# A retention block and two MoE layers on one core: the first layer by Strassen's algorithm over blocks of 768 tokens, all attention placed in front of it, and the weights' lowest three bits made by ScalarE from bytes

## The chip, the core and the metric

The kernel runs on 1 core of one Trainium2 chip. The metric is device time of one execution in microseconds (us). The core's engines are PE (TensorE: matmuls, with PEld for its weight loads), DVE (VectorE), ACT (ScalarE), POOL (GpSimd) and SP (SyncE), which issues most of the DMAs here.

## The reference

Three stages follow each other, over 2304 tokens of 512 features (4 sequences of 576 tokens, 8 heads of 64):

```python
def _attn_ref(q, k, v):
    scores = scale * np.matmul(q, k.transpose(0, 1, 3, 2))
    ...
    Dmat = np.where(rel >= 0, gamma[:, None, None] ** rel[None, :, :], 0.0)
    return np.matmul(scores * Dmat, v)

def _moe_ref(x, w_gate, w_val, w_out, rms_g):      # layer A: 512 -> 1536 -> 512
    rms = np.sqrt(np.mean(x * x, axis=-1, keepdims=True) + 1e-06)
    xn = x / rms * rms_g
    g = xn @ w_gate
    silu = g * (1.0 / (1.0 + np.exp(-g)))
    return silu * (xn @ w_val) @ w_out

def _moe2_ref(x, w_in, w_out):                     # layer B: 512 -> 2048 -> 512
    h = x @ w_in
    g = np.where(h >= 1, h, np.where(h <= -1, 0.0, (h + 1) ** 2 / 4))
    return g @ w_out
```

The weights arrive as float64 and are made into float32 on the chip.

## The kernel before

**Matmuls.** A float32 product is made of three matmuls in the type fp32r (`three`): every operand is cut into a rounded part hi and a rest lo, and hi·hi, lo·hi and hi·lo are summed in PSUM. Cutting (`split`) costs one ACT cast and one DVE subtraction. Attention and the norm's sums use plain fp32 matmuls; each shows as two records in the trace.

**Attention** (`scores`, `values`) goes through 20 chunks: per sequence four of 128 tokens and a tail of 64. It keeps a running state for each sequence, which DVE adds to and the next chunk reads. POOL makes the scaled q and k (`qs`, `ks`) and two sums of squares (`sq`, `sum`) for each chunk. The first chunks run in front; the other 13 are put between the matmuls of layer A by `att_step`, one half of a chunk after each front product.

**Layer A** runs in `BLOCKS` of 512, 512, 384, 512 and 384 tokens, with 12 steps (`step_a`) each, one for 128 of the 1536 hidden columns. A step has 24 front matmuls (gate and value: 2 outputs x 4 pieces of 128 features x 3) and, for the step before, 12 back matmuls, all as wide as the block. That makes 60 steps. In block 0 `weights_f32` converts three slots of weights for each step and stores them as float32 in DRAM; later blocks load them back, and every step splits them again.

**Conversion** (`convert`) of a slot of 128x512 weights: an ACT Prelu takes the high words, DVE shifts the result left by 3 (TENSOR_SCALAR), and DVE ors in the top three bits of the low word (SCALAR_TENSOR_TENSOR).

**Layer B** runs in three blocks of 768 tokens with 8 steps (`step_b`) each by Strassen's algorithm in Winograd's form: 2x2 blocks (384 tokens, two 128-column tiles, two halves of 256 features) take 7 products instead of 8, 42 matmuls of 384 columns, and 36 back matmuls of 512. Its weights' seven combinations are prepared during layer A (`prepare_in`, `prepare_out`) and loaded from DRAM.

**Order.** `Plan` records every operation and issues them in an order of its own: it steps through a schedule with costs for each operation, takes on PE the first ready operation in program order, and on the other engines the one due first. What runs on the chip is then that order on each engine, with semaphores for the real dependences. The lines below set what a step of layer A can wait for (two buffers for float32 weights, two for split ones, three staging slots) and when a new chunk of attention is begun.

```python
    w_p = pool("w", 2)
    wt_p = pool("wt", 2)
    stages = [stage_p.tile([P, DM, 2], U32, tag="stage", name="st") for _ in range(STAGE)]
    ...
        elif nscored[0] < min(len(chunks), goal + 1) and nscored[0] == nvalued[0]:
            scores(tags)
```

Of the kernel before, what the change touches and what calls it, by code (L numbers as in the profile page):

```python
# [12 lines left out]
U32 = mybir.dt.uint32  # L13
ACTF = mybir.ActivationFunctionType
# [6 lines left out]
P = 128  # L21
# [8 lines left out]
BLOCKS = [512, 512, 384, 512, 384]  # L30
STARTS = [sum(BLOCKS[:i]) for i in range(len(BLOCKS))]
TB = 384
NSB = NT // (2 * TB)
NPB = NB // 2
MT = 2 * TB // P
EPS = 1e-6
WARM = 16
AHEAD = 3
NORM = NA - 3
ATT = 3  # L40
STAGE = 3
PREPARE = [(), (1, 3, 5, 7), (5, 7), (1, 3, 5, 7), (0, 1, 2, 3, 5, 6)]
# [18 lines left out]
class Plan:  # L61
# [49 lines left out]
    def take(self, engine, real, method, args, kwargs):  # L111
# [10 lines left out]
        for ap, write in [(a, False) for a in ins] + [(out, True)]:  # L122
# [89 lines left out]
def moe_chain_kernel(ctx: ExitStack, tc: tile.TileContext, att, tail, wa, wb, dmat, gq, gk, out):  # L212
    nc = Plan(tc.nc)
    pool = lambda name, bufs, **k: Ring(ctx.enter_context(tc.tile_pool(name=name, bufs=1, **k)), bufs)

    const = pool("const", 1)
    att_p = pool("att", ATT)
    qk_p = pool("qk", 1)
    ret_p = pool("ret", 1)
    stage_p = pool("stage", STAGE)  # L220
    w_p = pool("w", 2)
    wt_p = pool("wt", 2)
    one_p = pool("one", 1)
    h_p = pool("h", 3)
    xraw_p = pool("xraw", 2)
    t_p = pool("t", 2)
    r_p = pool("r", 1)
    sum_p = pool("sum", 2)
    sq_p = pool("sq", 1)
    ps_p = pool("ps", 1, space=PSUM)  # L230
    fr_p = pool("fr", 2, space=PSUM)
    dram_p = pool("dram", 1, space=DRAM)
    d_sb = const.tile([P, H, CH], F32, name="d_sb")
    gq_sb = const.tile([P, NPAIR * (S - CH)], F32, name="gq_sb")
    gk_sb = const.tile([P, NFULL * H + KD], F32, name="gk_sb")
    rg_sb = gk_sb[:, NFULL * H:]
    eps = const.tile([P, 1], F32, name="eps")
    ones = const.tile([P, P], F32, name="ones")
    ones_r = const.tile([P, P], F32R, name="ones_r")
    state = const.tile([P, NPAIR, P], F32, name="state")  # L240
    o_sb = one_p.tile([P, 2 * DM], F32, name="o")
# [12 lines left out]

    def need(t):
        end = STARTS[t] + BLOCKS[t]
        return sum(b * S + c * CH < end for b in range(B) for c in range(NCH))


    slots = [wa[f, :, j * DM:(j + 1) * DM] for f in range(NA) for j in range(3)]  # L260
    slots += [wb[p, k, j] for p in range(NPB) for k in range(2) for j in range(2)]
    stage_t, loaded, taken = {}, [0], [0]
    stages = [stage_p.tile([P, DM, 2], U32, tag="stage", name="st") for _ in range(STAGE)]
    more = [*stages, *(a.rearrange("p (n w) -> p n w", w=2) for a in (wpair_w, wsum_w))]
    stage_of = [more[i % len(more)] if 9 <= i < 3 * NA - 2 else stages[i % STAGE] for i in range(len(slots))]

    def load_slot():
        i = loaded[0]
        if i < len(slots):
            st = stage_of[i]  # L270
            assert all(st is not b for b in stage_t.values())
# [26 lines left out]
    w32_t, wt_t = {}, {}  # L298

    def weights_f32(s):  # L300

        if s >= len(steps):
            return
        f = steps[s][2]
        w = w32_t[s] = w_p.tile([P, 3 * DM], F32, tag="w", name="w")
        if s < NA:
            convert(w, 3)
            nc.sync.dma_start(out=wa32[f], in_=w)
        else:
            nc.sync.dma_start(out=w, in_=wa32[f])  # L310

    def weights_split(s, part):
        if s >= len(steps):
            return
        if part == 0:
            wt_t[s] = wt_p.tile([P, 14 * 2 * P], F32R, tag="wt", name="wt") if s + 1 < len(steps) else wprep
        q = slice(0, 2 * DM) if part == 0 else slice(2 * DM, 3 * DM)
        hi, lo = wt_t[s][:, :3 * DM], wt_t[s][:, 3 * DM:6 * DM]
        split(w32_t[s][:, q], hi[:, q], lo[:, q])

    def a_weights(s, j):
        hi, lo = wt_t[s][:, :3 * DM], wt_t[s][:, 3 * DM:6 * DM]
        return hi[:, j * DM:(j + 1) * DM], lo[:, j * DM:(j + 1) * DM]

    def prepare_in(p):

        convert(wpair, 2)
        n = 2 * P
        a11, a12, a21, a22 = (wpair[:, i * n:(i + 1) * n] for i in range(4))
        s2, s1, s3, s4 = (wsum[:, i * n:(i + 1) * n] for i in range(4))  # L330
# [4 lines left out]
        ready = wprep[:, :14 * n]  # L335
# [4 lines left out]
        nc.sync.dma_start(out=wfd[p], in_=ready.bitcast(F32))  # L340

    def prepare_out(p):
        convert(wpair, 2)
        hl = wprep[:, :4 * DM].rearrange("p (f w n) -> p f w n", f=2, w=2)
        split(wpair.rearrange("p (f n) -> p f n", f=2), hl[:, :, 0], hl[:, :, 1])
        for f in range(2):
            nc.sync.dma_start(out=wod[p, f], in_=wprep[:, f * 2 * DM:(f + 1) * 2 * DM].bitcast(F32))

    prepared = [0]

    def prepare():
        i = prepared[0]
        if i < 2 * NPB:
            (prepare_out if i % 2 else prepare_in)(i // 2)
            prepared[0] += 1

    chunks = [(b, c) for b in range(B) for c in range(NCH)]
    first, ahead = need(0), need(0) + AHEAD  # L360
# [167 lines left out]
    def split_x(t, k0, k1):  # L528
# [9 lines left out]
        if k1 == KD:  # L538
            del xraw[t]
# [351 lines left out]
```

## Time and profile before

| | |
|---|---|
| median of 3 runs | 920.0 us (919.15 to 921.18) |
| the profiled execution | span 920.9 us, granted TensorE clock 0.998 of full speed |
| PE busy | 904.3 us, 98% of the span |
| DVE busy | 576.2 us (63%): between 20 and 340 us 78 to 97% of each 20 us, in layer B 32 to 69% |
| ACT busy | 482.3 us (52%) |
| POOL busy | 70.3 us, all in the first 400 us |
| DMA | 209.9 MB, mean 228 GB/s; 397 GB/s in the busiest stretch |

The span of the profiled execution stands 0.9 us above the median of the runs. PE's busy time counts matmuls that wait in the pipeline as well, so 98% does not mean that no faster order exists; it means that after the opening hardly a gap is left, and that time is decided by what PE is given to do.

### The profile page before, as it was taken

To read this page: it belongs to the slowest core of one execution; us is meant where nothing else is said; L and a number is where in the kernel's file an instruction comes from. 1 tells how busy PE (TensorE), PEld (TensorE's weight loads), DVE (VectorE), ACT (ScalarE), POOL (GpSimd) and SP (SyncE) were. 2 spreads that over 40 slices of the span, in tenths; PEclk is the share of its full clock that TensorE was granted. 3 is DMA by queue.
4 is the path that set the end of the run, shared out by engine and by line. 5 is a ranking of instruction groups with operands and counts; after the bars stand their busy time and mean duration, and the time that the engine had idled before them with its cause. 6 is when DMAs were issued, how large, how long until landed. Compare 5 with 4: busy or idle time off the path is not lost.

```text
span 920.9 us, 13342 instructions
## 1 busy us (share of the span) xinstructions
PE 904.3 (98%) x5098; PEld 797.7 (87%) x5098; DVE 576.2 (63%) x929; ACT 482.3 (52%) x858; POOL 70.3 (8%) x80
## 2 busy tenths in 40 slices
PE   8799999999999999999999999999999999999998
PEld 7578888888889998888899998989888998989896
DVE  3978888888988888855658645434734345434343
ACT  3446665555765576533545454445654455644443
POOL 4620001310014001100000000000000000000000
PEclk9999999999999999999999999999999999999999
DMA  9679976988769984642254386646765454755432
GB/s 364 229 261 314 308 278 235 331 331 325 283 240 378 387 291 150 234 150 94 103 202 153 104 329 243 216 160 216 251 222 194 169 191 170 266 165 213 159 137 69
DMA packets 51647, 209.94 MB, mean 228 GB/s; under 512 B 5632, under 2 KB 11392, under 8 KB 47488
## 3 DMA queue, kind: packets, MB, share of 16 engines
q1 hardware_dynamic: 45392, 199.51, 61.2%
q10 hardware_dynamic: 6192, 9.59, 2.8%
q8 instruction: 40, 0.66, 0.3%
q14 instruction: 23, 0.19, 0.1%
HBM read 167.14 MB, written 41.94 MB: 227 GB/s over the span
## 4 chain that ended last, share of the span: by engine, by line
PE 92%; DVE 4%; DMA 2%; ACT 2%; issue 1%; ACTq 0%
PE fr L135 50%; PE acc L135 31%; PE at L135 11%; DMA out_dram<-o 1%; DMA att<-in_att_dram 1%; DVE xraw L135 1%; DVE xall L135 0%; DVE t L135 0%; DMA gk_sb<-in_gk_dram 0%; DVE w L135 0%; DVE wt L135 0%; ACT att L135 0%; DVE state L135 0%; DVE wsum L135 0%; DVE wpair L135 0%
## 5 line engine op out<-in xcount | busy, mean ns | idle before, releaser
L135 PE MATMUL fr<-xall,wt 128*128 128x384 f32 (+1 forms) x2424 | 512.1, 356 | 3.6 <-DVE xall L135 1.3
L135 PEld LDWEIGHTS fr<-xall,wt 128*128 128x128 f32 x2424 | 436.8, 188 | 53.5 <-DVE xall L135 2.4
L135 PE MATMUL acc<-h,wt 128*128 128x512 f32 (+1 forms) x708 | 158.1, 370 | 0.1
L135 PE MATMUL acc<-wprep,h 128*128 128x512 f32 x576 | 155.7, 394 | 0.5 <-ACT h L135 0.5
L135 PEld LDWEIGHTS acc<-h,wt 128*128 128x128 f32 x708 | 128.4, 188 | 18.2 <-ACT o L135 0.6
L135 DVE TENSOR_TENSOR wt<-w,wt 128x512 fp32r<-128x512 f32 (+1 forms) x118 | 114.4, 985 | 17.7 <-ACT wt L135 17.3
L135 PEld LDWEIGHTS acc<-wprep,h 128*128 128x128 f32 x576 | 106.6, 188 | 15.8 <-ACT h L135 0.9
L135 ACT CAST wt<-w 128x512 fp32r<-128x512 f32 (+1 forms) x118 | 96.7, 835 | 42.1 <-PE acc L135 23.6
L135 DVE TENSOR_TENSOR t<-fr,t 128x512 f32<-128x512 f32 (+1 forms) x120 | 76.3, 636 | 58.0 <-PE fr L135 29.5
L135 ACT ACTIVATE att<-att 128x384 f32<-128x384 f32 x156 | 79.2, 523 | 30.1 <-DVE att L135 18.2
L135 ACT CAST h<-t 128x512 fp32r<-128x512 f32 (+1 forms) x60 | 34.6, 577 | 79.3 <-DVE t L135 79.3
L135 DVE TENSOR_TENSOR att<-fr,att 128x384 f32<-128x384 f32 x48 | 26.6, 555 | 70.6 <-ACT att L135 69.6
L135 PE MATMUL at<-wprep,h 128*128 128x512 f32 x288 | 70.3, 392 | 0.0
L135 DVE TENSOR_TENSOR h<-att,h 128x384 fp32r<-128x384 f32 x96 | 52.8, 554 | 23.7 <-ACT h L135 23.1
L135 ACT ACTIVATE t<-fr 128x512 f32<-128x512 f32 (+1 forms) x60 | 33.3, 554 | 59.0 <-PE fr L135 58.7
L135 PEld LDWEIGHTS at<-wprep,h 128*128 128x128 f32 x288 | 53.7, 188 | 10.4
L135 ACT COPY att<-fr 128x384 f32<-128x384 f32 x48 | 23.0, 479 | 75.7 <-PE fr L135 70.2
L135 ACT CAST h<-att 128x384 fp32r<-128x384 f32 x96 | 48.7, 512 | 21.2 <-DVE att L135 20.0
L135 DVE SCALAR_TENSOR_TENSOR att<-att,att 128x384 f32<-128x384 f32 x48 | 26.8, 558 | 42.3 <-ACT att L135 42.3
L135 DVE TENSOR_TENSOR h<-t,h 128x512 fp32r<-128x512 f32 (+1 forms) x60 | 38.0, 634 | 14.2 <-ACT h L135 13.9
L135 DVE SCALAR_TENSOR_TENSOR att<-att,fr 128x384 f32<-128x384 f32 x24 | 13.3, 553 | 36.8 <-ACT att L135 36.8
L135 DVE TENSOR_TENSOR xall<-xraw,xall 128x512 fp32r<-128x512 f32 (+2 forms) x32 | 25.9, 828 | 2.8 <-ACT xall L135 2.4
(144 smaller groups left out, 672.5 us busy)
## 6 DMA issues: line engine op xcount, KB each, us to landing
w<-wa SPq DMA_DIRECT2D x48, 768.0 KB, 4.5
wprep<-wod SPq DMA_DIRECT2D x48, 512.0 KB, 4.0
wt<-wfd SPq DMA_DIRECT2D x24, 1024.0 KB, 5.2
wt<-wfd SPq DMA_DIRECT2D x24, 768.0 KB, 4.5
stage<-in_wb_dram SPq DMA_DIRECT2D x32, 512.0 KB, 6.4
wfd<-wprep SPq DMA_DIRECT2D x8, 1792.0 KB, 7.0
att<-in_att_dram SPq DMA_DIRECT2D x26, 512.0 KB, 5.8
stage<-in_wa_dram SPq DMA_DIRECT2D x26, 512.0 KB, 5.5
```

Of the source, the lines that this page charges most:

```text
L135: call = lambda: getattr(real, method)(*args, **kwargs)
```

## The change

- **Layer A in 768-token blocks, by the algorithm of layer B.** There are 3 blocks of 12 steps. A step makes gate and value together by 7 products (42 matmuls of 384 columns), and its back part is 12 matmuls of 512 columns and 12 of 256, in accumulators that are 768 tokens wide (`acc0` to `acc3`, and the halves of `at0` and `at1`).
- **Weights of layer A** are prepared like those of layer B: in block 0 each step converts its three slots, makes four sums, splits seven combinations into the buffer `wt` and stores the split ones (1792 KB) and the plain out-weights (256 KB); blocks 1 and 2 load them.
- **Attention in front**, with sequences taken in pairs (0 and 1, then 2 and 3, chunk by chunk in turn). The state of a sequence adds up in a PSUM bank (`fr0`, `fr1`) and ACT copies it out, so DVE adds no more to it. x of the first 768 tokens stays on the chip; x of the others goes to DRAM (`x1d`) and comes back once in each block.
- **Conversion**: ACT makes the low word's top three bits from its top byte (Identity with scale and a bias, written over the staged low words), and one DVE operation shifts and ors. The TENSOR_SCALAR is gone.
- **Silu** replaces Sigmoid and one multiplication. Sums for the norm are made with all three blocks in or just behind the front, so ACT loads its tables 4 times in place of 11.
- **Layer B** keeps its steps. The weights of its steps 3, 5 and 7 (`LATE`) are converted and split within its own first block, the others during blocks 1 and 2 of layer A.

```diff
-BLOCKS = [512, 512, 384, 512, 384]
-PREPARE = [(), (1, 3, 5, 7), (5, 7), (1, 3, 5, 7), (0, 1, 2, 3, 5, 6)]
+ATT = 6
+LATE = (3, 5, 7)
...
-            nc.vector.tensor_scalar(out=q, in0=q, scalar1=3, scalar2=None, op0=ALU.logical_shift_left)
-            nc.vector.scalar_tensor_tensor(
-                out=q, in0=st[:, :, 0], scalar=29, in1=q, op0=ALU.logical_shift_right, op1=ALU.bitwise_or
-            )
+        for q, st in parts:
+            low = st.bitcast(U8).rearrange("p n (w b) -> p n w b", w=2)[:, :, 0, 3]
+            nc.scalar.activation(out=st[:, :, 0], in_=low, func=ACTF.Identity, scale=2.0 ** -5, bias=half)
+            nc.vector.scalar_tensor_tensor(
+                out=q, in0=q, scalar=3, in1=st[:, :, 0], op0=ALU.logical_shift_left, op1=ALU.bitwise_or
+            )
             load_slot()
...
+    def prepare_front(ready, dst):
+        convert(wpair_w)
...
         nc.vector.tensor_add(out=s1, in0=a21, in1=a22)
         nc.vector.tensor_sub(out=s2, in0=s1, in1=a11)
         nc.vector.tensor_sub(out=s3, in0=a11, in1=a21)
         nc.vector.tensor_sub(out=s4, in0=a12, in1=s2)
...
+    def prepare_a(s):
+        prepare_front(wts[s % 2], None)
+        w = w32o[s % 2]
+        convert(w)
+        w = w.bitcast(F32)
+        split(w, wos[s % 4][:, :DM], wos[s % 4][:, DM:])
...
+    def store_a(s):
+        nc.sync.dma_start(out=wfa[s], in_=wts[s % 2].bitcast(F32))
+        nc.sync.dma_start(out=woa[s], in_=w32o[s % 2].bitcast(F32))
...
-    chunks = [(b, c) for b in range(B) for c in range(NCH)]
+    chunks = [(b, c) for pair in ((0, 1), (2, 3)) for c in range(NCH) for b in pair]
...
             for h in range(2):
                 r = slice(h * D, (h + 1) * D)
-                if c:
-                    nc.vector.tensor_add(out=state[r, :, r], in0=state[r, :, r], in1=new[r])
-                else:
-                    nc.scalar.copy(out=state[r, :, r], in_=new[r])
+                nc.scalar.copy(out=st[r, :, r], in_=new[r])
...
+    def step_a(s):
+        b, f = divmod(s, NA)
+        if s + 1 < NA:
+            with nc.later_than(marks[-4] if s == 0 else None):
+                prepare_a(s + 1)
+        units = back_a(s - 1) if s else []
...
+        product(w, 0, d, True, False)
...
+        p1 = temp("p1", 1)
+        nc.scalar.copy(out=p1, in_=d)
+        product(w, 1, x, True, True)
+        after(1)
+        c = temp("c", 2)
+        nc.vector.tensor_add(out=c, in0=x, in1=p1)
+        g0 = gated(c)
+        product(w, 2, d, False, False)
...
+        product(w, 4, d, False, False)
+        after(4)
+        u3 = temp("u3", 2)
+        nc.scalar.copy(out=u3, in_=d)
+        nc.vector.tensor_add(out=u3, in0=x, in1=u3)
+        fill(2)
+        product(w, 5, x, False, True)
...
+        if s >= NA and s % 2:
+            limit[0] = len(slots)
+            with nc.later_than(len(nc.ops) - 1):
+                prepare_b()
```

The back part's units in the new `step_a`, in the order in which `fill` takes them (the 256-column ones first):

```python
        def part(d, wide):
            ps, q = (big[d], slice(0, 512)) if wide else (small[d], slice(512, SB))
...
        return [lambda d=d, wide=wide: part(d, wide) for wide in (False, True) for d in range(KD)]
```

**What moves.** On PE, before, in the middle of layer A (block 1): rows of attention (`at` from `qs`, `state`, `ret`) stand between the 12 matmuls of gate (`fr_138`) and of value (`fr_139`).

```order
L135 MATMUL fr_138<-xall_113,wt_151 128x512 x12
L135 MATMUL at_0_144<-qs_135,state_111 128x64 x4
L135 MATMUL at_0_144<-ret_0_133,att_125 64x64
L135 MATMUL at_0_144<-ret_0_134,att_125 64x64
...
L135 MATMUL fr_139<-xall_113,wt_151 128x512 x12
L135 MATMUL at_0_144<-att_126 128x128 x4
L135 MATMUL acc_0_142<-h_153,wt_152 128x512 x3
L135 MATMUL acc_0_143<-h_153,wt_152 128x512 x3
```

On PE, of the change, the end of attention (`at_94`, `at_95` are the banks `at0`, `at1`; `fr_100`, `fr_101` are `fr0`, `fr1`, here those of layer A's step 0):

```order
L137 MATMUL acc_99<-att_84 64x64 x4
L137 MATMUL fr_100<-xall,wt_64 128x384 x3
L137 MATMUL at_95<-prep,state 128x128 x4
L137 MATMUL at_95<-prep,att_87 64x128 x8
L137 MATMUL fr_100<-xall,wt_64 128x384 x3
L137 MATMUL fr_101<-xall,wt_64 128x384 x5
L137 MATMUL at_94<-prep,state 128x64 x4
L137 MATMUL at_94<-prep,att_89 64x64 x8
L137 MATMUL fr_101<-xall,wt_64 128x384
L137 MATMUL fr_100<-xall,wt_64 128x384 x6
L137 MATMUL at_95<-prep,state 128x64 x4
L137 MATMUL at_95<-prep,att_85 64x64 x8
```

All of attention now stands ahead of layer A, but for 18 matmuls of step 0 that are put among its last rows.

On PE, before, one step of layer A (24 front, 12 back matmuls):

```order
L135 MATMUL fr_138<-xall_113,wt_151 128x512 x12
L135 MATMUL fr_139<-xall_113,wt_151 128x512 x12
L135 MATMUL acc_0_142<-h_155,wt_152 128x512 x3
L135 MATMUL acc_0_143<-h_155,wt_152 128x512 x3
L135 MATMUL acc_0_140<-h_155,wt_152 128x512 x3
L135 MATMUL acc_0_141<-h_155,wt_152 128x512 x3
```

On PE, of the change, the middle of one step in block 0:

```order
L137 MATMUL fr_100<-xall,wt_64 128x384 x6
L137 MATMUL at_94<-h_69,wo 128x256 x2
L137 MATMUL at_95<-h_69,wo 128x256 x2
L137 MATMUL fr_100<-xall,wt_64 128x384
L137 MATMUL at_94<-h_69,wo 128x256 x4
L137 MATMUL fr_101<-xall,wt_64 128x384 x6
L137 MATMUL at_95<-h_69,wo 128x256 x4
L137 MATMUL fr_100<-xall,wt_64 128x384 x5
L137 MATMUL acc_96<-h_69,wo 128x512 x3
L137 MATMUL acc_97<-h_69,wo 128x512 x3
```

Products of six matmuls take turns with back matmuls of 256 and 512 columns, where there were runs of 24 and 12.

On DVE, before, eight rows in a row from a step of block 0 (`t` is what comes of gate and value, `w` converted weights):

```order
L135 TENSOR_TENSOR wt_151<-w_149,wt_151 128x512
L135 TENSOR_TENSOR wt_152<-w_150,wt_152 128x1024
L135 TENSOR_SCALAR w_149<-w_149 128x512
L135 TENSOR_TENSOR t_0_129<-fr_138,t_0_129 128x512
L135 SCALAR_TENSOR_TENSOR w_149<-stage_121,w_149 128x512
L135 TENSOR_SCALAR w_149<-w_149 128x512
L135 TENSOR_TENSOR t_0_131<-fr_139,t_0_129 128x512
L135 SCALAR_TENSOR_TENSOR w_149<-stage_122,w_149 128x512
```

On DVE, of the change, ten rows in a row from a step of block 0 (`att_84` to `att_89` are layer A's temporaries, `w32o` the out-weights):

```order
L137 SCALAR_TENSOR_TENSOR wpair<-wpair,stage_75 128x512
L137 TENSOR_TENSOR dg<-xraw,dg 128x768
L137 TENSOR_TENSOR wt_64<-wpair,wt_64 128x2x256
L137 SCALAR_TENSOR_TENSOR wpair<-wpair,stage_76 128x512
L137 TENSOR_TENSOR att_85<-fr_100,att_85 128x384
L137 TENSOR_TENSOR wsum<-wpair 128x256 x2
L137 TENSOR_TENSOR wsum<-wsum,wpair 128x256
L137 SCALAR_TENSOR_TENSOR w32o_74<-w32o_74,stage_77 128x512
L137 TENSOR_TENSOR wsum<-wpair,wsum 128x256
L137 TENSOR_TENSOR att_86<-fr_100,att_86 128x384
```

The sums of weights (`wsum`) and the additions on what the products leave (`att_85`, `att_86` from `fr`) are new on DVE here; the shift is gone.

## Rows read from the trace of the kernel before

**Rows 1.** The page: busy us, share of the span and instructions of each engine
```profile
PE 904.3 (98%) x5098; PEld 797.7 (87%) x5098; DVE 576.2 (63%) x929; ACT 482.3 (52%) x858; POOL 70.3 (8%) x80
```

**Rows 2.** The chain that ended last, in order of time: start us, us, what
```profile
411.05 5.44 PE fr L135 x24
419.21 5.44 PE fr L135 x24
...
479.83 4.16 PE fr L135 x24
486.07 4.16 PE fr L135 x24
```

**Rows 3.** PE in order of time: start us, us, form, count, [idle before <-releaser]
```profile
10.95 1.13 PE L135 MATMUL at<-ret,att 128*64 128x128 f32 x16 [2.19 <-DMA att<-in_att_dram]
...
22.45 1.16 PE L135 MATMUL at<-t,state 128*128 128x128 f32 x8 [0.97 <-DVE state L135]
```

**Rows 4.** PE in order of time: the first matmuls of layer B
```profile
537.22 3.28 PE L135 MATMUL fr<-xall,wt 128*128 128x384 f32 x18
```

**Rows 5.** PE in order of time: eight fp32 records with 128 columns of weights
```profile
46.07 1.06 PE L135 MATMUL at<-t,state 128*128 128x128 f32 x8
```

**Rows 6.** Groups by form: weight loads; busy us, mean ns | idle before
```profile
L135 PEld LDWEIGHTS fr<-xall,wt 128*128 128x128 f32 x2424 | 436.8, 188 | 53.5 <-DVE xall L135 2.4 <-ACT d_sb L135 1.5 <-DVE att L135 1.4
```

**Rows 7.** Groups by form: POOL; busy us, mean ns | idle before
```profile
L135 POOL TENSOR_TENSOR sq<-sq 128x256 f32<-128x256 f32 x14 | 14.0, 998 | 12.7 <-ACT sq L135 12.7
L135 POOL TENSOR_TENSOR qs<-att,gq_sb 128x512 f32<-128x512 f32 x8 | 11.5, 1435 | 76.5 <-PE at L135 65.5 <-issue 4.5 <-PE acc L135 3.6
L135 POOL TENSOR_TENSOR ks<-att,gk_sb 128x512 f32<-128x512 f32 x10 | 11.4, 1140 | 29.5 <-DMA att<-in_att_dram 25.2 <-PE at L135 4.3
L135 POOL TENSOR_TENSOR sum<-sq 128x128 f32<-128x128 f32 x14 | 8.3, 593 | 0.9
```

**Rows 8.** Groups by form: DVE
```profile
L135 DVE TENSOR_TENSOR att<-fr,att 128x384 f32<-128x384 f32 x48 | 26.6, 555 | 70.6 <-ACT att L135 69.6 <-PE fr L135 1.0
L135 DVE SCALAR_TENSOR_TENSOR w<-stage,w 128x512 uint32<-128x512 uint32 x26 | 17.6, 685 | 0.1
L135 DVE TENSOR_SCALAR w<-w 128x512 uint32<-128x512 uint32 x36 | 16.1, 458 | 7.7 <-ACT w L135 7.3
L135 DVE TENSOR_TENSOR wprep<-wsum,wprep 128x1024 fp32r<-128x1024 f32 x8 | 11.1, 1393 | 0.5 <-ACT wprep L135 0.4
L135 DVE TENSOR_TENSOR wsum<-wpair 128x256 f32<-128x256 f32 x16 | 7.2, 468 | 0.1
L135 DVE TENSOR_TENSOR wprep<-wpair,wprep 128x512 fp32r<-128x512 f32 x8 | 5.5, 681 | 0.0
```

**Rows 9.** Groups by form: ACT
```profile
L135 ACT ACTIVATE att<-att 128x384 f32<-128x384 f32 x156 | 79.2, 523 | 30.1 <-DVE att L135 18.2 <-DVE h L135 10.1 <-ACT o L135 0.4
L135 ACT COPY att<-fr 128x384 f32<-128x384 f32 x48 | 23.0, 479 | 75.7 <-PE fr L135 70.2 <-DMA out_dram<-o 4.4
L135 ACT ACTIVATE w<-stage 128x512 f32<-128x512 f32 x26 | 17.0, 669 | 10.5 <-DMA wa<-w 5.4 <-DMA stage<-in_wa_dram 4.3 <-DVE w L135 0.7
L135 ACT CAST wprep<-wsum 128x1024 fp32r<-128x1024 f32 x8 | 8.4, 1047 | 1.2 <-DMA x2d<-o 1.2
L135 ACT CAST wprep<-wpair 128x512 fp32r<-128x512 f32 x8 | 5.0, 619 | 3.6 <-DVE wpair L135 3.6
```

**Rows 10.** Stretches (us): PE, PEld, DVE, ACT, POOL busy us (instructions), PE clock, DMA share, GB/s
```profile
80.00:100.00 20.00, 20.00 (x89) 16.27 (x88) 18.11 (x32) 12.66 (x21) 0.00 (x0) 1.00 0.94 325
180.00:200.00 20.00, 20.00 (x139) 16.37 (x138) 19.33 (x31) 9.69 (x16) 4.17 (x5) 1.00 0.99 378
300.00:320.00 20.00, 19.48 (x123) 18.52 (x122) 17.06 (x26) 13.22 (x20) 1.11 (x1) 1.00 0.98 397
```

**Rows 11.** DMA issues: KB each, median us from issue to landing
```profile
stage<-in_wa_dram SPq DMA_DIRECT2D x26, 512.0 KB, 5.5
```

**Rows 12.** The page: bytes moved, GB/s in 40 slices
```profile
GB/s 364 229 261 314 308 278 235 331 331 325 283 240 378 387 291 150 234 150 94 103 202 153 104 329 243 216 160 216 251 222 194 169 191 170 266 165 213 159 137 69
```

More of the change, by code (lines that the diff above doesn't have):

```diff
@@ L213, in moe_chain_kernel @@
     nc = Plan(tc.nc)
[L214 to L229, printed above, removed]
@@ L263, in moe_chain_kernel @@
-    stages = [stage_p.tile([P, DM, 2], U32, tag="stage", name="st") for _ in range(STAGE)]
-    more = [*stages, *(a.rearrange("p (n w) -> p n w", w=2) for a in (wpair_w, wsum_w))]
-    stage_of = [more[i % len(more)] if 9 <= i < 3 * NA - 2 else stages[i % STAGE] for i in range(len(slots))]
+    one = ctx.enter_context(tc.tile_pool(name="one", bufs=1))
+    psum = ctx.enter_context(tc.tile_pool(name="psum", bufs=1, space=PSUM))
+    dram = ctx.enter_context(tc.tile_pool(name="dram", bufs=1, space=DRAM))
@@ new lines, in moe_chain_kernel @@
+    stages = [one.tile([P, DM, 2], U32, name=f"stage{i}")[:, :, :] for i in range(STAGE)]
+    ss = sb("ss", NT)
+    o_sb = sb("o", 3 * DM)
+    gk_sb = sb("gk_sb", NFULL * H + KD)
+    eps = sb("eps", 1)
+    half = sb("half", 1)
+    ones = sb("ones", P)
+    atts = [sb(f"att{i}", 8 * CH) for i in range(ATT)]
+    prep = sb("prep", 8 * DM)
+    dg = sb("dg", H * CH + NPAIR * (S - CH))
+    states = sb("state", 2 * NPAIR * P)
+    xout = sb("xout", 3 * DM)
+    banks = {n: psum.tile([P, 512], F32, name=n)[:, :] for n in ("at0", "at1", "acc0", "acc1", "acc2", "acc3", "fr0", "fr1")}
@@ new lines, in moe_chain_kernel, with split @@
+    gq_sb = dg[:, H * CH:]
+    state = [a.rearrange("p (u n) -> p u n", u=NPAIR) for a in cut(states, NPAIR * P)]
+    x_j = [a.rearrange("p (k n) -> p k n", k=KD) for a in cut(xraw, KD * TB)]
+    def split(src, hi, lo):
+        nc.scalar.copy(out=hi, in_=src)
+        nc.vector.tensor_sub(out=lo, in0=src, in1=hi.bitcast(F32))
+    slots = [wa[f, :, j * DM:(j + 1) * DM] for f in range(NA) for j in range(3)]
+    slots += [wb[p, k, j] for p in EARLY + LATE for k in range(2) for j in range(2)]
@@ L560, in back_a @@
-    def back_a(s, i):
-        _, t, f = steps[s]
-        T = BLOCKS[t]
-        oh, ol = a_weights(s, 2)
-        hh, hl = h_t[s]
-        if f == 0 and i == 0:
-            acc_t[t] = [ps_p.tile([P, 512], F32, tag=f"acc{i}") for i in range(KD)]
-        ps = acc_t[t][i]
-        q = slice(i * P, (i + 1) * P)
-        three(ps[:, :T], oh[:, q], ol[:, q], hh[:, :T], hl[:, :T], f == 0, f == NA - 1)
-        if f == NA - 1:
-            o = next(o_next)
-            nc.scalar.copy(out=o[:, :T], in_=ps[:, :T])
-            nc.scalar.dma_start(out=x2d[:, i, STARTS[t]:STARTS[t] + T], in_=o[:, :T])
@@ L820, in moe_chain_kernel @@
-    for j in range(4, 7):
-        split_xb(0, j)
+    for _ in range(WARM):
+        nc.tensor.matmul(banks["fr0"][:, :P], lhsT=ones, rhs=ones, start=True, stop=True)
+    tags = itertools.cycle((("acc0", "acc1"), ("acc2", "acc3")))
+    ready = [max(i for i, (b, c) in enumerate(chunks) if b * S + c * CH < (k + 1) * SB) for k in range(NSB)]
+    marks = []
+    for i in range(len(chunks) + 1):
+        if i < len(chunks):
+            scores(i, next(tags))
+        marks.append(len(nc.ops) - 1)
+        if i:
+            values(i - 1)
+        for k in range(NSB - 1):
+            if ready[k] == i - 1:
+                rms(k, next(tags))
+                if k == 0:
+                    norm(0)
+                    sums_x(True)
+        if i == 4:
+            with nc.later_than(marks[2]):
+                prepare_a(0)
```

597 lines of the change are left out of this document (268 added, 329 removed).

## The prediction

> **What bounds the kernel now.** I read the page first: PE is busy for 98% of the span [rows 1], so what counts is how much work it is given and how long it stands in the opening. The chain in order of time then gives the price of that work: in layer A the chain is PE alone, and one step follows the other after 8.16 us with 512 tokens and 6.24 us with 384 [rows 2]. A step has 36 matmuls, so one of 512 columns takes 0.2267 us and one of 384 takes 0.1733 us; 128 columns cost 0.0534 us and 0.013 us is fixed. With 36 steps of the first kind and 24 of the second, layer A's matmuls take 36 x 8.16 + 24 x 6.24 = 443.5 us. Layer B begins at 537.2 us [rows 4]; the last back part of layer A (12 x 0.1733 = 2.1 us) lies behind that. So 537.2 - 441.4 = 95.8 us before layer B are attention and waits, and layer B with the end of the kernel takes 920.9 - 537.2 = 383.7 us, 2.1 of them layer A's. The other engines don't bind, though DVE is close to it: it is busy 18.1 to 19.3 of 20 us in stretches where PE has no gap, and where it is at 17.1 with DMA at 397 GB/s PE loses half a microsecond [rows 10].
>
> **Layer A's matmuls.** A step now has 42 matmuls of 384 columns (7.28 us), 12 of 512 (2.72 us) and 12 of 256. No fp32r matmul of 256 columns is in the trace. By the line through the other two it takes 0.1733 - 0.0534 = 0.120 us. From below, its columns alone are 0.107 us. From above, each matmul loads 128 columns of weights of its own: eight fp32 records with such weights pass in 1.06 us [rows 5], so a load needs at most 0.133 us. Far above lies the mean length of a load, 0.188 us [rows 6], which would count if loads could not overlap; rows 5 speak against that, and with matmuls of 0.1733 us the loads of 0.188 us must overlap as well. I take 0.120: a step is 7.28 + 2.72 + 1.44 = 11.44 us, 36 of them 411.9 us. That is 31.6 us less than before, 5.6 us either way between 0.107 and 0.133, and 29 us of the gain would be lost at 0.188.
>
> The Trainium skill (TensorE: Matmul & The Clock Gate, LDWEIGHTS) has a load take its columns divided by 1.2 GHz, which gives an estimate of 107 ns for 128 columns: by it the 256-column matmul is bound by its own columns, and the total stays at 889 us; by the row's 188 ns as a rate it would be 919 us. The trace agrees with the page in that eight loads pass in 1.06 us.
>
> **Attention in front.** PE has no layer A to fill its waits with now, so the slowest of the others sets the pace. POOL is that: a full chunk costs it 1.435 + 1.140 + 0.998 + 0.593 = 4.17 us [rows 7], 12 times; the first chunk of each of the four sequences has no `qs` (2.73 us), and a tail has no `ks` and half the columns (I take two thirds of the rest, 2.0 us). That is 50.0 + 10.9 + 8.1 = 69 us; the page has 70.3 us for all of POOL [rows 1]. Before, the first values begin at 10.95 us [rows 3]; `ks` must be there by then, so POOL begins near 9.8 us. Without a gap attention would end at 79 us; at 93% of POOL's time at 84 us, which I take, since two sequences in turn and a state that PSUM adds up remove the wait of one chunk for the last. From below: the values of the first four chunks follow each other after (22.45 - 10.95)/3 = 3.83 us though each waits for the state before [rows 3], which gives 10.95 + 15 x 3.83 + 4 x 2 = 76 us. From above: in the front some 26 MB move (20 chunks, constants, weights of two steps, 1536 tokens of x written out); at 278 GB/s, a middling slice of the opening [rows 12], that is 94 us. 18 matmuls of step 0 stand ahead of the last attention rows, as the order shows: 3.1 us come off.
>
> **Block 0: weights.** Each step converts three slots, sums and splits. On DVE: 3 x 0.685 (shift and or), 4 x 0.468 (sums), splits 1.393 + 0.681 + 0.681 + 0.468, and seven operations of 0.555 on what PE leaves: 11.0 us [rows 8]. The three shifts of 0.458 us are gone, but the sums and four operations on the products came. On ACT: 3 x 0.669 for the high words, 3 for the bytes, casts 1.047 + 0.619 + 0.619 + 0.479, copies 3 x 0.479, and four of 0.523: 10.3 us [rows 9], if a byte operation costs what its neighbour on the same staged words costs (0.669). No row shows one; from below a 512-wide cast has 0.619, from above I take twice 0.669 for bytes read and words written 8 bytes apart, and ACT is at 12.3 us, over PE's. Against 11.44 us of PE, DVE stands at 96% and ACT at 90%. Nothing is left to cover what comes late: the copy of product 0 has one product (1.04 us) until product 2 needs its bank; it takes 0.479 us, but may queue behind a cast of 1.05 us, and behind it wait Silu and the gate's splits. In layer B six back matmuls lie in that place. The weights' own circle is no bound: a slot lands after 5.5 us [rows 11], then 0.67 + 0.67 + 0.69 us make it whole and the splits that free its target fit under the next load, some 8 us in all. Between nothing (rows 10 show DVE at 97% with PE full) and 2 us per step I take 0.8, nearer the row with a gap than the full ones because ACT is full too: 9 us over 11 steps. Step 1's weights are still being split while step 0 runs: 2 us. Twice, x of the next block is split (seven 768-wide splits, near 1 us each on DVE) within one step: 2 us each. Together 15 us, with 5 and 30 as ends.
>
> **Edits at nothing.** Blocks 1 and 2 have DVE at 3.9 us a step for the products plus 0.7 for the out-weights, and every second step 6 us for layer B's weights: PE hides all. Fewer table loads and Silu take work from ACT where it had time. `LATE` adds about 5 us to ACT and 6 to DVE in six steps of layer B, which take 383.7/24 = 16 us each and have eleven operations of 0.555 us on DVE (6.1) and three of 0.479 and twelve of 0.523 on ACT (7.7) [rows 8, 9]; without that cover it would be 6 us for each of the six. Layer B keeps its matmuls.
>
> **The sum**, against the profiled execution of 920.9 us: front 84 - 3.1, layer A 411.9 of which the last back part (12 x 0.2267 + 12 x 0.120 = 4.2) falls behind the border, so 407.7, late things 15, layer B with the end 383.7 - 2.1 + 4.2 = 385.8: 889.4 us. What is not layer A's matmuls comes to 95.9 us where it was 95.8: attention in front saves nothing by itself, and all the gain is Strassen's. The execution is 0.9 us above the median of the runs, so 889 us for that.
>
> **Rivals.**
> *Block 0 bound by DVE and ACT.* For it: 96% and 90%, and the dear byte operation. At 2.0 to 3.0 us over PE per step it is 902 to 914 us. Against it: rows 10, where a full DVE leaves PE dense.
> *Block 0 bound by DMA, slower than before.* A step moves 1.5 MiB of slots in and 2.0 MiB of split and plain weights out, 3.67 MB. `wt` has two buffers and cannot be rewritten before its store has landed, and the slots queue behind that store on SP. At 325 GB/s [rows 10] this takes 11.3 us and hides; at 229 GB/s, the opening's low [rows 12], 16.0 us: 4.6 x 12 - 9 = 46 us more, 935 us. It decides from 14.8 us a step on, 248 GB/s. Against it: 378 and 397 GB/s were moved when asked for [rows 10].
> *Loads of 0.188 us bind the 256-column matmuls*: 919 us, no change.
> *A front slower by 10 to 20 us*, held by DMA and three chunks' buffers: 899 to 909 us.
> *Better*: front 76, late things 5: 871 us.
>
> **How the numbers follow.** Forecast (876 to 904) 0.58; better 0.08; DVE and ACT 0.14; DMA 0.10; 256 columns 0.04; front 0.06. The predicted time is 889 us. The range from 873 to 918 takes in all but half of better, DMA's case and half of the 256-column one, some 0.16. A change of 0.2%, 1.8 us, is about what a measurement of this kernel can tell from none. Faster by more than that: 0.87, all but DMA's and the 256 columns' case with a little of these; within it 0.04; slower 0.09.
>
> **What would show it.** Right: `at<-h,wo` with 256 columns every 0.12 us; steps of blocks 1 and 2 every 11.4 us and those of block 0 about 12.2, with DVE over 90%; POOL busy for 69 us up to about 85; layer B's first product near 505 us, and from there 386 us. Wrong: PE waiting for `wt` in block 0 with DMA or `stage` as releaser (DMA), steps of 13 us with ACT or DVE without gap, `at` waiting for `xout` or `att` loads in front, or 0.19 us for a 256-column matmul.

## The result and the profile after

The changed kernel takes 898.3 us (median of 4 runs, 897.5 to 900.0) where the kernel before, on the same chip, takes 920.0 us: a ratio of 0.976, 95% interval 0.975 to 0.978. The forecast was 889 us. The profiled execution has a span of 898.2 us; it is the slowest of the four and the one read below.

The page of the changed kernel, engines' busy time (compare [rows 1]):
```profile
PE 881.7 (98%) x5316; PEld 807.0 (90%) x5316; DVE 536.0 (60%) x916; ACT 528.6 (59%) x1025; POOL 70.4 (8%) x76
```
PE has less work and is as full as before; ACT has more, as the bytes and the copies of products ask. The chain in order of time gives layer A's price again (compare [rows 2]); each row here is the first three products of a step:
```profile
292.81 3.14 PE fr L137 x18
...
304.43 3.14 PE fr L137 x18
...
315.97 3.14 PE fr L137 x18
```
Steps of block 1 follow each other after 11.62 and 11.54 us (11.44 forecast). The groups by form show the two prices that no row of before had:
```profile
L137 PE MATMUL at<-h,wo 128*128 128x256 f32 x432 | 65.5, 282 | 1.3 <-ACT h L137 1.3
L137 ACT ACTIVATE stage<-stage,half 128x512 uint32<-128x512 uint8 x68 | 50.6, 765 | 0.0
```
The mean of 282 ns is the length of one pipelined matmul, not its price: from start to start of two neighbours it is 120 ns (median 118 ns). The byte operation takes 0.765 us, where I took 0.669.

PE in order of time, at the three borders of the sum (attention's last values, step 2's first product, layer B's first product; compare [rows 4]):
```profile
95.50 0.68 PE L137 MATMUL at<-prep,att 64*64 64x64 f32 x16
...
115.37 3.39 PE L137 MATMUL fr<-xall,wt 128*128 128x384 f32 x18 [0.57 <-DVE att L137]
...
513.29 1.92 PE L137 MATMUL fr<-xall,wt 128*128 128x384 f32 x10
```
Attention's last matmul starts at 96.0 us, which is taken as its end here and below; 84 was forecast. From there to layer B it is 417.3 us (419.6 forecast), from there to the end 384.9 us (385.8). So 12.0 us were lost in the front, 2.3 and 0.9 us came back behind it: 8.8 us, the whole miss against the 889.4 us of the sum.

The stretches of the front, one of block 0 and one of block 1 (columns as in [rows 10]):
```profile
0.00:20.00 20.00, 16.79 (x184) 15.38 (x186) 5.63 (x12) 5.08 (x10) 8.61 (x13) 0.91 0.92 357
20.00:40.00 20.00, 18.00 (x272) 15.96 (x266) 13.14 (x17) 13.93 (x28) 16.85 (x18) 1.00 0.98 345
40.00:60.00 20.00, 19.00 (x272) 15.63 (x273) 16.51 (x22) 10.49 (x23) 16.75 (x18) 1.00 0.85 293
60.00:80.00 20.00, 16.99 (x191) 14.30 (x189) 18.54 (x20) 10.07 (x18) 17.20 (x15) 0.83 0.64 199
80.00:100.00 20.00, 19.22 (x193) 17.13 (x194) 11.96 (x22) 16.27 (x31) 10.96 (x14) 1.00 0.77 263
120.00:140.00 20.00, 20.00 (x114) 18.94 (x114) 18.25 (x34) 14.45 (x27) 0.00 (x0) 1.00 0.90 329
320.00:340.00 20.00, 20.00 (x113) 18.82 (x113) 9.83 (x17) 9.62 (x19) 0.00 (x0) 1.00 0.96 366
```
Block 0 is dense on PE though DVE is at 91%. In the front PE is not: from 60 to 80 us it has 191 instructions where 20 to 40 us have 272, DVE and POOL are both near full, and the granted clock falls to a mean of 0.83. PE and ACT there, in order of time:
```profile
59.73 1.16 PE L137 MATMUL acc<-att 64*128 64x128 f32 x16
63.58 2.05 PE L137 MATMUL at<-prep,state 128*128 128x128 f32 x8 [2.68 <-ACT xout L137]
```
```profile
61.58 0.60 ACT L137 ACTIVATE xout<-at 128x512 f32<-128x512 f32 x1 [2.83 <-POOL ss L137]
62.08 0.74 ACT L137 COPY state<-fr 64x256 f32<-64x256 f32 x2
62.84 0.59 ACT L137 COPY xout<-at 128x512 f32<-128x512 f32 x1
```
PE waits 2.7 us for ACT, which waits 2.8 us for POOL to have added the squares of an earlier chunk (`sq`, a part of `xout`, is one buffer). Eight records that took 1.06 us [rows 5] then take 2.05: PE is granted its lower level, 1.2 GHz, from about 63.1 to 69.9 us, as it was from 11.9 to 15.3 us.

The four executions tell what these stretches can be worth. This one was granted 0.994 of full speed in the mean; the others were granted 0.996, 0.998 and 1.000 and have spans of 896.4, 896.6 and 895.7 us. Even with the full clock 6.3 of the 8.8 us remain, so the half clock accounts for at most some 2.5 us.

### The profile page after: what moved, and what is told of

Same layout as the page of the kernel before. It is cut to its first block, busy times and chain, and to the rows that moved or that the text cites. A ratio compares the mean times of both kernels' runs of the same rounds, so it can differ in the third digit from the quotient of the medians.

```text
span 898.2 us, 14044 instructions
## 1 busy us (share of the span) xinstructions
PE 881.7 (98%) x5316; PEld 807.0 (90%) x5316; DVE 536.0 (60%) x916; ACT 528.6 (59%) x1025; POOL 70.4 (8%) x76
## 4 chain that ended last, share of the span: by engine, by line
PE 91%; ACT 2%; POOL 2%; issue 2%; DVE 1%; DMA 1%; ACTq 0%; POOLq 0%; DVEq 0%
PE fr L137 49%; PE acc L137 27%; PE at L137 16%; POOL prep L137 1%; DMA att<-in_att_dram 1%; POOL xout L137 1%; ACT att L137 1%; POOL ss L137 1%; DMA gk_sb<-in_gk_dram 0%; DVE wsum L137 0%; DVE wt L137 0%; ACT xout L137 0%; DVE att L137 0%; ACT stage L137 0%; ACT wt L137 0%
## 5 line engine op out<-in xcount | busy, mean ns | idle before, releaser
L137 PE MATMUL fr<-xall,wt 128*128 128x384 f32 x2520 | 499.1, 337 | 2.0 <-ACT att L137 1.0
L137 DVE TENSOR_TENSOR att<-fr,att 128x384 f32<-128x384 f32 x216 | 119.9, 557 | 164.3 <-ACT att L137 105.0
L137 ACT COPY att<-fr 128x384 f32<-128x384 f32 x180 | 86.0, 478 | 136.3 <-PE fr L137 133.2
L137 PE MATMUL acc<-wo,h 128*128 128x512 f32 x576 | 154.6, 393 | 0.5 <-ACT h L137 0.5
L137 PEld LDWEIGHTS acc<-wo,h 128*128 128x128 f32 x576 | 106.8, 188 | 16.3 <-ACT h L137 0.9
L137 PE MATMUL acc<-h,wo 128*128 128x512 f32 x432 | 116.7, 394 | 0.0
L137 PEld LDWEIGHTS acc<-h,wo 128*128 128x128 f32 x432 | 79.7, 188 | 10.6
L137 PE MATMUL at<-wo,h 128*128 128x512 f32 x288 | 70.1, 392 | 0.0
L137 PE MATMUL at<-h,wo 128*128 128x256 f32 x432 | 65.5, 282 | 1.3 <-ACT h L137 1.3
L137 PEld LDWEIGHTS at<-h,wo 128*128 128x128 f32 x432 | 61.3, 188 | 3.1 <-ACT h L137 2.7
L137 PEld LDWEIGHTS at<-wo,h 128*128 128x128 f32 x288 | 53.7, 188 | 10.4
```

## The experiments

Times are medians, ratios are to the kernel before on the same chip; the changed kernel's is 0.976 (0.975 to 0.978). "Attention's end" is that of the profiled execution (96.0 us in the changed kernel). PE ran products of layer A ahead of it, 0.1733 us each; without these 18 it is 92.9 us. That "net" time compares the fronts. Every edit also makes `Plan` choose its order anew (0 to 24 products stand ahead of attention's end in the experiments), so a few us between two runs can't be put to the edit alone.

**1. What is Strassen worth: an eighth product.** Each step of layer A adds product 3 twice.
```diff
         product(w, 3, x, True, False)
+        product(w, 3, x, False, False)
```


> The changed kernel with one product more in each step of layer A (product 3 is summed twice: six matmuls of 384 columns, the count of the plain algorithm, with no more work on any other engine). Theory 'PE bounds all of layer A': 36 x 6 x 0.1735 = 37 us more, 935 to 936. Theory 'block 0 is bound by DVE and ACT': its 12 steps hide most of it, 24 x 1.04 = 25 us and a little, 922 to 926.

Measured 933.3 us, ratio 1.014 (1.012 to 1.016): 35 us over the changed kernel, where 36 x 6 x 0.1733 = 37.4 us were added to PE. From step 2 on the steps of all three blocks follow each other after some 12.6 us. Layer A is bound by PE's matmuls, and with eight products this kernel is slower than before.

**2. A second buffer for the squares**, since the row at 61.58 us names it.
```diff
-        sq = xout[:, 2 * DM:2 * DM + NPAIR * n].rearrange("p (u n) -> p u n", n=n)
+        sq = (xout[:, 2 * DM:], w32o[1].bitcast(F32))[i % 2][:, :NPAIR * n].rearrange("p (u n) -> p u n", n=n)
```


> The changed kernel with a second buffer for a chunk's squares (the out-weights' second buffer, free in front), used in turn. Theory 'ACT waits for POOL': with one buffer ACT's Square of a chunk waits for POOL's two sums of the chunk before, and the copies queued behind it on ACT hold the banks that PE needs; attention should end 4 to 8 us earlier than 96 us, time 890 to 894. Theory 'POOL's own work': POOL is 84% busy between its first and last full chunk, its work is unchanged, so at most 2 us, 896 to 898.

Measured 900.1 us, 0.977 (0.976 to 0.979): no gain, net end 95.1 us. The wait named by the row went and others of 2.1 and 1.6 us came, up to 61.8 and 36.7 us, both ended by POOL's factors (`prep`). The longest wait was a place where the delay showed, not its cause.

**3. POOL's additions on DVE**, with the second buffer.
```diff
-        nc.gpsimd.tensor_add(out=sq[:, :2], in0=sq[:, :2], in1=sq[:, 2:])
-        nc.gpsimd.tensor_add(out=ss[:, g0:g0 + n], in0=sq[:, 0], in1=sq[:, 1])
+        nc.vector.tensor_add(out=sq[:, :2], in0=sq[:, :2], in1=sq[:, 2:])
+        nc.vector.tensor_add(out=ss[:, g0:g0 + n], in0=sq[:, 0], in1=sq[:, 1])
```


> The kernel with two buffers for squares, and both sums of squares moved from POOL to DVE: POOL's work falls from 70 to about 40 us, DVE gets about 13 us more in front. Theory 'POOL's own work': attention ends 8 to 14 us earlier, at 82 to 88 us, where PE's own 60 us of attention and the start at 11 us begin to bind; time 884 to 890. Theory 'PE and loads': POOL had room, at most 3 us better than the run with two buffers. Theory 'DVE is the next': DVE at 82 to 93% in 40 to 80 us gets over-full, no gain, 895 to 900.

Measured 901.2 us, 0.978 (0.975 to 0.982), net end 94.0 us, with POOL busy for 39.7 us in place of 70.4. DVE has the additions now, so this run alone doesn't acquit POOL; with experiment 9, which leaves them out altogether and gains nothing either, it shows that POOL's pace, the step on which my 84 us rested, does not set the front.

**4. Loads left out** for attention's chunks 6 to 19, which compute on what lies in the buffers.
```diff
-        if c < NFULL:
+        if i >= 12:
+            pass
+        elif c < NFULL:
```


> The changed kernel without the loads of attention's chunks 6 to 19: they compute with what the first six chunks left in the buffers, so about 13 MB less come in during the front. Theory 'loads': 26 MB at 290 GB/s take 90 us, so attention ends 10 us or more earlier, time below 889. Theory 'POOL' (its work or ACT's wait for it): at most 2 us, 896 to 898.

Measured 898.2 us, 0.977 (0.974 to 0.981), net end 90.4 us: the 2.5 us in the profile don't show in the time, and DMA alone isn't it either.

**5. All of POOL's work left out**, with these loads: q and k go in as loaded, `ss` is a constant.
```diff
-            nc.gpsimd.tensor_mul(out=qs, in0=qT, in1=gq_of(c).rearrange("p (u n) -> p u n", n=n))
+            qs_t[i] = qT
...
-            nc.gpsimd.tensor_mul(out=ks, in0=kt, in1=scale.unsqueeze(2).to_broadcast([P, H, D]))
+            ks_t[i] = att_t[2 * i + 1][:, :H * D].rearrange("p (h d) -> p h d", d=D)
...
-        nc.scalar.activation(out=sq, in_=x[:, :, :n], func=ACTF.Square)
-        nc.gpsimd.tensor_add(out=sq[:, :2], in0=sq[:, :2], in1=sq[:, 2:])
-        nc.gpsimd.tensor_add(out=ss[:, g0:g0 + n], in0=sq[:, 0], in1=sq[:, 1])
```

> Leaves out, besides the loads of attention's chunks 6 to 19, everything that POOL does for a chunk: the factors on q and k (q and k are used as loaded), and the squares with their sums (ss is a constant), so that ACT's squares go too. PE, DVE and the copies keep their work. Theory 'POOL's pace, as forecast': attention ends 10 us or more earlier (84 to 86 us instead of 96), the kernel takes 886 to 890 us. Theory 'waits that move from engine to engine, half clock and PE's own work': 2 to 6 us, 893 to 897 us.

Measured 881.9 us, 0.958 (0.956 to 0.960). Attention ends at 75.6 us with all of PE's matmuls, and no stretch after the first wait is below full clock. PE in order of time, the last chunks:
```profile
72.42 1.10 PE L137 MATMUL at<-att,state 128*128 128x64 f32 x8
73.46 0.68 PE L137 MATMUL at<-prep,att 64*64 64x64 f32 x16
74.07 1.10 PE L137 MATMUL at<-att,state 128*128 128x64 f32 x8
75.11 0.68 PE L137 MATMUL at<-prep,att 64*64 64x64 f32 x16
75.72 2.35 PE L137 MATMUL fr<-xall,wt 128*128 128x384 f32 x12
```
The gain that I expected by the first theory (886 to 890 us) was too small, and the second theory fell by far: the cause is on POOL or beside it, though neither its additions moved to DVE nor the loads left out gained by themselves.

**6. Less PE work: six of eight heads' values left out** in the chunks that have a state.
```diff
-        for u, h, r in heads:
+        for u, h, r in heads[:2] if c else heads:
             nc.tensor.matmul(
                 x[r, u, :n], lhsT=v[:, 2 * u + h], rhs=ret[h][:n, u, :n],
```


> Leaves out six of the eight heads' products of the scores with v in the 12 full chunks and 4 tails that have a state: 12 records of 0.064 us a full chunk, 11 us of PE in all; POOL, DVE, ACT and the loads keep their work, and the waits on them stay. Theory 'PE's own work sets the front': 8 to 11 us less, 887 to 891 us. Theory 'PE waits for the others': 0 to 3 us, 896 to 899 us, with longer waits of PE in the front.

Measured 900.6 us, 0.979 (0.976 to 0.982), net end 92.0 us; its stretch from 60 to 80 us:
```profile
60.00:80.00 20.00, 14.93 (x154) 11.55 (x151) 18.51 (x20) 10.27 (x18) 15.74 (x15) 0.83 0.56 183
```
The expected 11 us less for PE became waiting of PE and half clock (17.0 us at the lower level in the front, 10.2 in the changed kernel). It is not PE's own work.

**7. Waits filled with matmuls of ones** to keep the clock up, eight each ahead of the values of chunks 8 and 12.
```diff
+        if i - 1 in (8, 12):
+            for _ in range(8):
+                nc.tensor.matmul(
+                    banks[f"fr{chunks[i - 1][0] % 2}"][:, 256:256 + P], lhsT=ones, rhs=ones, start=False, stop=False,
+                    skip_group_check=True,
+                )
         if i:
             values(i - 1)
```

> Nothing is left out; 16 matmuls of ones into unused columns of a bank stand ahead of the values of chunks 8 and 12, 3.4 us of PE where it waited 1.3 and 2.9 us. Theory 'the half clock after a wait costs the front': no stretch at half clock before 90 us, 2 to 4 us less, 894 to 897 us. Theory 'the clock is no matter, or falls elsewhere': the fillers cost what no wait hides, 898 to 902 us.

Measured 902.6 us, 0.980 (0.979 to 0.982): slower by some 3 us, about what the fillers take (3.4 us expected). The clock fell all the same (0.89 in 60 to 80 us, 0.85 in 80 to 100): the longest wait, now 4.5 us, ends at 78.5 us, behind the fillers. This run shows no worth of the clock.

**8. Block 0's operands left out** (DVE's scaling, sums and splits, ACT's casts; a constant in their place).
```diff
-                if k == 0:
-                    norm(0)
-                    sums_x(True)
```


> Leaves out what DVE and ACT do to make block 0's operands between 45 and 85 us: the four scalings by norm and gain, the four sums and the seven splits, some 16 us of DVE and 8 us of ACT; the operands are a constant written at the start. Theory 'DVE full between 50 and 80 us holds the scores' results back': 5 to 10 us less, 888 to 893 us, without PE's wait of 2.9 us near 61 us. Theory 'that work stands beside PE's': 0 to 2 us, 896 to 898 us.

Measured 892.5 us, 0.970 (0.968 to 0.971), net end 86.7 us; the wait at 61 us shrank to 0.6 us, and the half clock behind it is gone. PE's wait ends at POOL and ACT, yet taking work from DVE (and casts from ACT) gains 6 us. The clock is a part of that: executions granted the full clock have spans of 890.5 and 890.7 us here and of 895.7 in the changed kernel, 5 us apart. And POOL's work, the same as before in amount, took 62.0 us in place of 70.4.

**9. Only the additions and squares left out**, and **10. only the factors** (with the loads of 4): the last three removed lines of the diff under 5 alone, or the others alone.

> Leaves out ACT's squares and POOL's two additions for each chunk (ss is a constant): 31 us of POOL and some 10 us of ACT; the factors on q and k stay on POOL. Theory 'POOL's pace': POOL has 39 us left, attention ends 10 us or more earlier, 885 to 890 us. Theory 'the factors' place between scores and values is what holds PE (q and k must be multiplied before the values can go)': 2 to 6 us, 892 to 896 us.

> Leaves out the loads of attention's chunks 6 to 19 (no change by itself) and POOL's multiplications of q and k by their factors, 40 us; squares and sums stay on ACT and POOL (31 us). Theory 'POOL's pace': as much as without the sums or more, 883 to 888 us. Theory 'the sums hold the banks of the values': 0 to 4 us, 894 to 898 us.

Without the additions 899.5 us, 0.978 (0.974 to 0.981), net end 92.1 us; without the factors 886.9 us, 0.963 (0.961 to 0.965), net end 79.1 us. Since the loads alone changed nothing, it is the 32 multiplications of q and k by their factors, 40 us of POOL, that cost 11 us, at least where the loads are out as well. The theory of POOL's pace would have had a gain from both runs: it got experiment 10's time and missed experiment 9's by 10 us.

**11. The lowest bits by DVE as before.**
```diff
-            low = st.bitcast(U8).rearrange("p n (w b) -> p n w b", w=2)[:, :, 0, 3]
-            nc.scalar.activation(out=st[:, :, 0], in_=low, func=ACTF.Identity, scale=2.0 ** -5, bias=half)
+            nc.vector.tensor_scalar(out=q, in0=q, scalar1=3, scalar2=None, op0=ALU.logical_shift_left)
             nc.vector.scalar_tensor_tensor(
-                out=q, in0=q, scalar=3, in1=st[:, :, 0], op0=ALU.logical_shift_left, op1=ALU.bitwise_or
+                out=q, in0=st[:, :, 0], scalar=29, in1=q, op0=ALU.logical_shift_right, op1=ALU.bitwise_or
```


> The lowest three bits as before: DVE shifts both words (one operation of 0.458 us more a slot, 1.4 us a step), ACT makes none from bytes (0.765 us less a slot). Theory 'DVE binds block 0': DVE goes from 92% to over 100% of a step of 11.7 us, 8 to 15 us more, 906 to 913 us. Theory 'hidden by PE': 0 to 2 us more, 898 to 900 us.

Measured 900.5 us, 0.979 (0.976 to 0.982), not to be told from the change. In block 0 PE is full, or nearly so, with either. With DVE's shift:
```profile
120.00:140.00 20.00, 20.00 (x116) 18.68 (x115) 18.24 (x36) 10.13 (x20) 0.00 (x0) 1.00 0.87 300
160.00:180.00 20.00, 20.00 (x113) 18.75 (x112) 18.52 (x38) 12.18 (x24) 0.00 (x0) 1.00 0.91 320
200.00:220.00 20.00, 20.00 (x117) 18.77 (x116) 17.93 (x36) 13.12 (x26) 0.00 (x0) 1.00 0.88 329
```
The changed kernel, besides the stretch from 120 us above:
```profile
160.00:180.00 20.00, 19.63 (x112) 18.28 (x111) 18.49 (x34) 15.17 (x28) 0.00 (x0) 1.00 0.83 288
200.00:220.00 20.00, 20.00 (x116) 18.83 (x115) 16.02 (x33) 15.71 (x30) 0.00 (x0) 1.00 0.79 301
```
The bytes on ACT free DVE of 0.42 us a slot and cost ACT 0.77 us; PE hides both: steps 2 to 11 take 117.0 us with DVE's shift and 117.2 without. My expectation had DVE over 100% there; the stretches show 90 to 93%.

**12. The factors shared**: DVE multiplies for chunks 2 to 5 and 16 to 19.
```diff
+        pool = nc.vector if 2 <= i < 6 or i >= 16 else nc.gpsimd
...
-            nc.gpsimd.tensor_mul(out=qs, in0=qT, in1=gq_of(c).rearrange("p (u n) -> p u n", n=n))
+            pool.tensor_mul(out=qs, in0=qT, in1=gq_of(c).rearrange("p (u n) -> p u n", n=n))
...
```


> Computes everything; for chunks 2 to 5 and 16 to 19 DVE multiplies q and k by their factors in place of POOL, some 0.6 us an operation for 1.1 to 1.4 us, 13 operations, where DVE was busy for a third to a half of the time. Theory 'POOL with DVE beside it paces the front': POOL's 70 us become 53, attention ends 3 to 6 us earlier, 892 to 895 us. Theory 'DVE's own work is what binds': no gain or a loss, 898 to 902 us.

Measured 897.6 us, 0.975 (0.973 to 0.977): the interval holds the changed kernel's 0.976. Net end 89.7 us in the profile, which the runs don't confirm as a gain. No run gave a version that beats the change.

## Why the prediction was right and where it failed

**What two engines do to each other.** In this kernel the tiles `at`, `acc` and `fr` lie in PSUM, where PE writes its results, and all others on the chip in SBUF. POOL in the changed kernel, in order of time, with all of its operands in SBUF:
```profile
61.51 1.27 POOL L137 TENSOR_TENSOR prep<-att,dg 128x512 f32<-128x512 f32 x1
...
64.45 0.73 POOL L137 TENSOR_TENSOR xout<-xout 128x256 f32<-128x256 f32 x1
65.26 1.05 POOL L137 TENSOR_TENSOR ss<-xout 128x128 f32<-128x128 f32 x1
66.27 1.99 POOL L137 TENSOR_TENSOR prep<-att,dg 128x512 f32<-128x512 f32 x1
68.33 1.33 POOL L137 TENSOR_TENSOR xout<-xout 128x256 f32<-128x256 f32 x1
```
DVE at the same time:
```profile
61.16 1.27 DVE L137 TENSOR_TENSOR prep<-acc,dg 128x512 f32<-128x512 f32 x2
...
63.51 1.28 DVE L137 TENSOR_TENSOR prep<-acc,dg 128x512 f32<-128x512 f32 x2
64.71 1.29 DVE L137 TENSOR_TENSOR xraw<-xraw 128x768 f32<-128x768 f32 x1
65.92 1.21 DVE L137 TENSOR_TENSOR xall<-xraw,xall 128x768 fp32r<-128x768 f32 x1
67.05 2.02 DVE L137 TENSOR_TENSOR xraw<-xraw 128x768 f32<-128x768 f32 x1
```
DVE without POOL (all of POOL left out), the same operations:
```profile
52.66 0.95 DVE L137 TENSOR_TENSOR xall<-xraw,xall 128x768 fp32r<-128x768 f32 x1
53.65 0.96 DVE L137 TENSOR_TENSOR xraw<-xraw 128x768 f32<-128x768 f32 x1
54.52 1.28 DVE L137 TENSOR_TENSOR prep<-acc,dg 128x512 f32<-128x512 f32 x2
```
An addition of 0.96 us takes up to 2.02 us, and the factor that takes 1.27 us beside the scores' multiplication takes 1.99 beside a split and an addition: each has the other's time in it, as if the one that starts second ran when the first is done (67.05 + 2.02 = 69.07 is the end of the factor, 68.26, and 0.81 more). The factor's 1.435 us of [rows 7] probably held such time already, as DVE worked beside POOL before too. The scores' multiplication, `prep<-acc,dg`, reads PSUM, and two of them take 1.27 or 1.28 us in either run; but it queues behind a DVE operation that waits for POOL, and PE can wait for it. Experiment 9, without additions, shows that (POOL, DVE and PE):
```profile
31.29 2.43 POOL L137 TENSOR_TENSOR prep<-att,dg 128x512 f32<-128x512 f32 x2
31.65 2.35 DVE L137 TENSOR_TENSOR wsum<-wpair 128x256 f32<-128x256 f32 x2
37.51 1.60 DVE L137 TENSOR_TENSOR prep<-acc,dg 128x512 f32<-128x512 f32 x3
38.24 0.43 PE L137 MATMUL at<-prep,att 128*64 128x128 f32 x2 [2.64 <-DVE prep L137]
```
Two sums of weights that take 0.42 us each without POOL take 2.35 us beside its factors, and PE then waits 2.6 us for the scores' multiplication, which stands behind them and other work on the weights in DVE's order. Over the changed kernel's front the four additions of `xraw` take 1.49 us in the mean where they take 0.95 alone, the seven splits 1.29 where 0.95.

The Trainium skill (SBUF — State Buffer, SBUF: two separate sides and Who interferes with whom) states that a DVE instruction with two SBUF inputs contends with a GpSimd instruction that reads SBUF, and that the first to issue keeps the pair of SBUF ports that the two engines share for its whole length. The trace agrees in these rows, and in that the multiplications with a PSUM operand are not lengthened (1.27 or 1.28 us for two in either run). By that rule work moved from POOL to DVE stays in the same queue, and experiments 3 and 12 moved such work.

The length of that queue is no bound by itself, though. From 8 us to attention's end, POOL's operations and DVE's with two SBUF inputs together cover 77 of 88 us in the changed kernel, 67 of 90 in experiment 3 and 61 of 88 in experiment 9 (estimates, added up from the traces' rows), and neither experiment gained. That leaves the question which operation stands behind which, and no run here changes that order alone.

**Point by point.** *The matmuls of layer A* came as forecast: 0.120 us for 256 columns, and 11.55 to 11.6 us a step in blocks 1 and 2. 0.19 us for a load as a bound fell. *Attention in front* is the step that failed: "the slowest of the others sets the pace. POOL is that", and 84 us from 69 us of POOL at 93%. POOL's amount was right (70.4 us), its pace was not the bound (experiments 3 and 9): the front is longer than any engine's work because PE waits in turn for POOL, DVE and ACT. That POOL and DVE take turns where I let them stand side by side is shown in the rows; how many of the 12 us it costs is not. Against the run with all of POOL left out, the net end is 17.3 us late: 8.0 us of it are PE's waits (starts over 0.33 us apart, less 0.22 us each: 10.9 us against 2.9), 3.4 us the 6.8 us at half clock, 1.7 us a like stretch in the first 20 us; the rest, 4.2 us, lies in smaller waits that I didn't single out. The clock's 5.1 us are a count and not a worth: by the four executions at most some 2.5 us would come back without them. The rival of a front slower by 10 to 20 us had the right time, 899 us, and the wrong cause, DMA and the chunks' buffers: without most of the loads, which wait for both, the time stayed (experiment 4). The prediction's own sign of being wrong in the front, `at` waiting for `xout`, came (the row at 63.58 us). That 898 us lies near 889 owes to 3.2 us that came back behind the front, and inside the range to its width: the front alone missed by 12.0 us.

*Late things* came to 12.7 us (417.3 + 3.1 - 407.7) where I took 15, with other parts: steps 0 and 1 lost 3.8 us (2 taken); steps 2 to 11 took 117.2 us, 2.8 over 11.44 each (9 taken); the three steps around each of the two changes of block 3.5 together (4 taken); and the other 18 steps of blocks 1 and 2 together 2.6, taken at nothing. 0.8 us a step for a full DVE and ACT was the mis-sized term: it measured 0.28. *Block 0 bound by DVE and ACT* fell, since DVE bears 0.42 us a slot more (experiment 11); *bound by DMA* fell, PE never waited for `wt` there. *Layer B* kept its time: 384.9 us with `LATE` in it.

**What stays open.** Without the additions (experiment 9) POOL has 31 us less and the front gains nothing. Its rows above show the factors and DVE still in each other's way. POOL also waited 22.5 us for loads of q and k in that run (11.3 us in the changed kernel, 10.4 of them at the opening), so loads may have taken the place. Factors kept with both loads and additions left out was not run, nor factors left out with the loads kept. How the 6 us of experiment 8 divide between DVE's operations and ACT's casts is open too, and so is how much of any of these gains comes from the new order that `Plan` chose.

## What to carry to other kernels

The busy time of the fullest engine forecasts a stage only if the engines run side by side and none waits for another in turn: lay the rows of two engines over each other in time and see whether operations that are long in one stand beside the other. The longest wait in a view is where the delay shows; removing its releaser (experiment 2) moves it. Stages that are full on PE, as layers A and B here, get nearly all of what Strassen's algorithm saves in matmuls; what the stage costs that PE does not fill has to be forecast from its chain of waits.

## What the runs showed of the hardware

A wait of 2.7 us of PE from 60.9 us on went with 6.8 us at 1.2 GHz (63.1 to 69.9 us in the changed kernel), although PE worked from 63.6 us on; without the factors (experiment 10) waits of 1.9 and 1.7 us, up to 64.6 and 87.7 us, were followed by no fall, and the full clock was granted throughout (mean 1.000). ACT reads bytes 8 bytes apart and writes words 8 bytes apart at 0.765 us for 512, 0.1 us over a float operation on the same staged words (0.669).
